# Early, parked products for two z2 tiles, with their weights loaded first: one core, attention plus gMLP

## The chip, the cores and the metric

The kernel runs on one core of one Trainium2 chip. Times are device microseconds of that core; one profiled execution's *span* is about 1.7 us shorter than its time. Engines: PE (TensorE matmul), PEld (weight load, overlapped with PE), DVE (VectorE), ACT (ScalarE), POOL (GpSimd), SP (the queue that issues most DMA). A ratio below is the mean time of one kernel's fast runs over the mean time of the fast runs of the kernel before in the same rounds, so it is not quite the ratio of the medians quoted. A run is called slow when it is over 1.5% above the fastest of its kernel.

## The reference, cut to what matters

```python
xn = layernorm(x)                          # x: 2048 x 512, 16 token tiles of 128
qkv = xn @ wqkv                            # windowed attention: 8 slots, dilation 2
z = gelu(xn @ w_in)                        # w_in: 512 x 1376
z1, z2 = z[..., :688], layernorm(z[..., 688:])
g = w_sp @ z2 + b_sp                       # w_sp: 2048 x 2048
out = x + attention(q, k, v) @ wo + (z1 * g) @ w_out
```

Every token tile is normalised, transposed to `xnT`, and multiplied by the q/k, v, z1 and z2 weights. A z2 tile goes from PSUM through gelu on ACT, with its sum, then a square with its sum, and is normalised later.

## The kernel before

The schedule is manual: each engine runs its instructions in program order. Token tile `4*tb + j` is tile `(j, tb)`; block `j` is the four tiles with that `j`. Only block 0's first two tiles go through first, since their x comes first. The parts that matter:

```python
# DMA issue order on SP (first x tiles ahead of this)
load_wqk(SP, 0)                     # half of the q/k weights, 512 KB
SP.dma_start(xall[:, 1], xblk[1])   # x block 1, 512 KB
load_wqk(SP, 1)                     # second half, 512 KB
for j in range(2, 4):
    SP.dma_start(xall[:, j], xblk[j])
SP.dma_start(w_z2[:], ...)          # 688 KB, last

def zmm(i, wz):                     # L207: 8 matmuls of 344 columns into one "mm" buffer
    pz = ps_mm.tile([P, 2, TBS], F32, name="pz", tag="mm")     # ps_mm has 3 buffers
    ...
def z2_gelu(i, pz):                 # L213, ACT, frees the PSUM buffer
def z2_sq(i):                       # L219, ACT
def z2s(j, tb):
    i = blk(j)[tb]
    z2_gelu(i, zmm(i, w_z2)); z2_sq(i)
def qk_mm(j, c):                    # L264 matmuls into an "mm" buffer, L269 copy on ACT
    pq = qk_tile(); qk_part(pq, j, c, 0, TB); qk_copy(pq, j, c)

warm_up(9)                          # matmuls on a constant tile
... # layernorm of tile (0,0)
tr_copy(t0[0], tr(t0[0])); warm_up(2)
tr_copy(t0[1], tr(t0[1]))
... # q/k products of blocks 0 and 1, layernorm of blocks 1 to 3 on DVE
z2s(0, 0)
z2s(0, 1)
for c in range(C):                  # four q/k products of block 2
    qk_mm(2, c)
... # logits, products on DVE (prod_c L287, prod_w L297), v, z1, then the g stage
```

## Time and profile before

Before the prediction: 210.8 us, median of 3 runs (210.47 to 211.88).

| what | value | from |
|---|---|---|
| PE busy | 202.7 us, 97% of the span | page, busy times |
| the chain before 11.34 us | DMA of the second q/k half, 6.68 us | chain of waits |
| the chain after it | PE, without a hole of note | chain of waits |
| two z2 tiles on PE | 2.41 us | chain of waits |
| gelu and square of one z2 tile on ACT | 1.63 us | ACT timeline |

Three lines of the page of the kernel before; the last gives the busy tenths of PE in 40 equal slices.

```profile
span 209.3 us, 4186 instructions
...
PE 202.7 (97%) x1727; PEld 121.3 (58%) x1731; DVE 176.9 (85%) x267; ACT 92.9 (44%) x148; POOL 5.7 (3%) x21
...
PE   7799999999999999999999999999999999999993
```

The chain of waits of the kernel before, in its first 40 us: start, duration, what, and the number of instructions merged.

```profile
4.61 6.68 DMA r_w<-in_A_wqkv_dram
11.29 0.05 issue
11.34 2.36 PE pq L264 x20
13.69 0.45 PE pt L193 x8
14.14 9.57 PE pq L264 x72
23.71 2.41 PE pz L207 x16
26.12 1.73 PE pq L264 x8
27.84 0.01 issue
27.85 5.34 PE pq L264 x24
```

From 11.34 us each PE piece begins where the last ended. The hole to fill lies before.

The ACT timeline of the kernel before (start, duration, instruction).

```profile
25.67 1.28 ACT L213 ACT_TABLE_LOAD   x1
26.96 0.74 ACT L213 ACTIVATE z<-pz 128x688 bf16<-128x688 f32 x1
...
28.61 0.72 ACT L213 ACTIVATE z<-pz 128x688 bf16<-128x688 f32 x1
...
30.23 0.99 ACT L269 CAST r_qk<-pq 128x1024 bf16<-128x1024 f32 x1
```

The first gelu ends, with its 0.19 us accumulator read from 27.60, at 27.79 us. PE's second q/k product of block 2 needs that buffer and starts at 27.85.

### The profile page before, as it was taken

The numbers are of one execution on the slowest core, as the hardware profiler recorded it, in microseconds if no ns is written. First come the engines' busy times: TensorE is split into PE (matmuls) and PEld (weight loads), VectorE is DVE, ScalarE is ACT, GpSimd is POOL, SyncE is SP. The second block draws the span as 40 slices with busy tenths as digits, with TensorE's granted clock in tenths as the row PEclk, the third lists the DMA queues.
The fourth block names the chain that finished last, engine by engine and source line by source line (L and its number), as shares of the span: only waits on it lengthen the run. The fifth ranks groups of instructions, "written<-read, shape, count | busy, mean of one in ns | idle before, by whom it ended". The sixth has DMA issues, their size and how long they took to land.

```text
span 209.3 us, 4186 instructions
## 1 busy us (share of the span) xinstructions
PE 202.7 (97%) x1727; PEld 121.3 (58%) x1731; DVE 176.9 (85%) x267; ACT 92.9 (44%) x148; POOL 5.7 (3%) x21
## 2 busy tenths in 40 slices
PE   7799999999999999999999999999999999999993
PEld 2578644545566566666666666456666446664441
DVE  3888997969999987999999999859999979991404
ACT  3475797788997897941431223102123102231000
POOL 7000001100000000000000000000000000000000
PEclk9999999999999999999999999999999999999999
DMA  4984556000000499799999776994833234424153
GB/s 132 326 281 66 101 94 232 0 0 3 0 3 0 103 179 210 146 280 216 177 191 218 129 161 145 147 194 150 126 76 89 47 94 150 47 45 89 51 152 100
DMA packets 66914, 25.91 MB, mean 124 GB/s; under 512 B 56080, under 2 KB 66768, under 8 KB 66768
## 3 DMA queue, kind: packets, MB, share of 16 engines
q1 hardware_dynamic: 66304, 25.20, 56.1%
q10 hardware_dynamic: 592, 0.46, 0.7%
q8 instruction: 13, 0.21, 0.4%
q14 instruction: 5, 0.04, 0.1%
HBM read 10.13 MB, written 2.10 MB: 58 GB/s over the span
## 4 chain that ended last, share of the span: by engine, by line
PE 93%; DMA 3%; SPq 2%; issue 1%; DVE 0%; DVEq 0%
PE pg L377 36%; PE pz L207 18%; PE pq L264 12%; PE po L430 7%; PE po L411 7%; PE pv L342 7%; PE pl L304 4%; DMA r_w<-in_A_wqkv_dram 3%; PE pa L430 1%; PE po L417 1%; SPq L138 1%; SPq L131 1%; SPq L147 0%; PE pt L193 0%; DVE r_qk L422 0%
## 5 line engine op out<-in xcount | busy, mean ns | idle before, releaser
L377 PE MATMUL pg<-z,r_qk 128*128 128x344 bf16 x512 | 76.8, 309 | 0.0
L377 PEld LDWEIGHTS <-r_qk 128*128 128x128 bf16 x512 | 50.0, 98 | 24.9 <-issue 0.4
L207 PE MATMUL pz<-w_z,xnT 128*128 128x344 bf16 x256 | 40.9, 309 | 0.0
L380 ACT ACTIVATE gs<-pg,b_col 128x688 bf16<-128x688 f32 x16 | 13.3, 832 | 57.0 <-PE pg L377 50.1
L353 DVE TENSOR_TENSOR r_pr<-r_x,r_w 128x2048 bf16<-128x2048 bf16 x32 | 38.1, 1221 | 0.3
L357 DVE TENSOR_TENSOR r_pr<-r_pr 128x2048 bf16<-128x2048 bf16 x28 | 33.8, 1219 | 0.1
L207 PEld LDWEIGHTS <-xnT 128*128 128x128 bf16 x256 | 24.6, 98 | 14.7 <-issue 2.0
L264 PE MATMUL pq<-xnT,r_w 128*128 128x256 bf16 (+1 forms) x176 | 29.4, 321 | 0.8 <-ACT xnT L197 0.7
L297 DVE TENSOR_TENSOR r_pr<-r_qk 128x2048 bf16<-128x2048 bf16 x24 | 27.5, 1218 | 2.8 <-ACT r_qk L269 2.8
L264 PEld LDWEIGHTS <-r_w 128*128 128x128 bf16 x176 | 16.8, 98 | 11.5 <-issue 1.8
L422 DVE TENSOR_TENSOR r_qk<-po,r_qk 128x512 bf16<-128x512 f32 x14 | 9.0, 686 | 15.6 <-PE po L430 15.6
L256 ACT ACTIVATE z1u<-pz 128x688 bf16<-128x688 f32 x16 | 11.9, 742 | 20.8 <-PE pz L207 20.7
L269 ACT CAST r_qk<-pq 128x1024 bf16<-128x1024 f32 x16 | 15.8, 1012 | 5.8 <-PE pq L264 4.3
L430 PE MATMUL po<-r_w,uT 128*128 128x512 bf16 x66 | 14.9, 379 | 0.6 <-issue 0.6
L342 PE MATMUL pv<-xnT,r_w 128*32 128x512 bf16 x256 | 14.7, 380 | 0.0
L411 PE MATMUL po<-r_lg,r_pr 32*128 32x512 bf16 x224 | 14.5, 375 | 0.0
L430 PEld LDWEIGHTS <-uT 128*128 128x128 bf16 x80 | 7.5, 98 | 10.2 <-issue 1.7
L175 DVE BATCH_NORM_STATS2 stats<-r_x 128x6 f32<-128x512 bf16 x16 | 10.8, 672 | 2.3 <-DMA r_x<-in_A_x_dram 2.1
L219 ACT ACTIVATE junk<-z 128x688 bf16<-128x688 bf16 x16 | 12.4, 778 | 0.5
L213 ACT ACTIVATE z<-pz 128x688 bf16<-128x688 f32 x16 | 11.8, 736 | 1.9 <-PE pz L207 1.9
L342 PEld LDWEIGHTS <-r_w 128*32 128x32 bf16 x256 | 9.5, 139 | 4.5 <-issue 0.3
L411 PEld LDWEIGHTS <-r_pr 32*128 32x128 bf16 x256 | 6.2, 93 | 7.7 <-issue 1.3
(67 smaller groups left out, 136.3 us busy)
## 6 DMA issues: line engine op xcount, KB each, us to landing
r_lg<-in_A_wo_dram SPq DMA_DIRECT2D x4, 512.0 KB, 9.0
r_qk<-in_A_x_dram SPq DMA_DIRECT2D x16, 128.0 KB, 2.2
out_dram<-r_qk SPq DMA_DIRECT2D x15, 128.0 KB, 1.7
r_x<-in_A_x_dram SPq DMA_DIRECT2D x3, 512.0 KB, 6.0
w_z<-in_B_w_in_dram SPq DMA_DIRECT2D x2, 688.0 KB, 5.3
r_w<-in_A_wqkv_dram SPq DMA_DIRECT2D x4, 256.0 KB, 6.4
r_w<-in_B_w_out_dram SPq DMA_DIRECT2D x1, 640.0 KB, 5.6
r_w<-in_A_wqkv_dram SPq DMA_DIRECT2D x1, 512.0 KB, 4.0
```

What stands on the lines that cost most here:

```text
L207: PE.matmul(pz[:, hh, 0:FHALF], xnT[:, kc, i * P:(i + 1) * P], wz[:, kc, hh * FHALF:(hh + 1) * FHALF], start=(kc == 0), stop=(kc == C - 1))
L219: A.activation(junk[:], z2[:, i, :], ACT.Square, accum_out=zsq[:, q:q + 1])
L264: PE.matmul(pq[:, s, b0 * P:b1 * P], wqk[:, kc, s * D + c * P:s * D + (c + 1) * P], xv[:, kc, b0:b1, j, :], start=(kc == 0), stop=(kc == C ...
L269: A.copy(dst[:, :, :, j, :], pq[:].rearrange("p s (b t) -> p s b t", b=TB))
L297: V.tensor_tensor(pr[g % 2][:, :, ww], q4, k4, ALU.mult)
L342: PE.matmul(pv[32 * tb:32 * tb + 32, dd, :], wv[:, kc, 2 * d2 + dd, :], xnT[:, kc, tb * TBS:(tb + 1) * TBS], start=(kc == 0), stop=(kc == ...
L353: V.tensor_tensor(pw_t[n], vp[:, :, off:off + P], a_sb[:, slot_w(w), ts].unsqueeze(1).broadcast_to([P, DH, P]), ALU.mult)
L357: V.tensor_tensor(pw_t[n] if dst is None else dst, pw_t[n], pw_t[m], ALU.add)
L377: PE.matmul(pg[:, hh, 0:FHALF], wsp[n % NWSP][:, k, :], z2[:, k, hh * FHALF:(hh + 1) * FHALF], start=(q == 0), stop=(q == NT - 1))
L380: A.activation(gs[:], pg[:, :, 0:FHALF], ACT.Identity, bias=b_col[:, i:i + 1])
L411: PE.matmul(pos[tb], op[32 * tb:32 * tb + 32, d, o * P:(o + 1) * P], wo_r[32 * tb:32 * tb + 32, d, :], start=(d == 0), stop=False, tile_po ...
L430: PE.matmul(pos[tb], uT[:, o % 2, m, tb * P:(tb + 1) * P], wout[:, m, :], start=False, stop=(m == MCH - 3))
```

## The change

The intent: PE has a hole while it waits for q/k weights. Load the z2 weights first, multiply the first two token tiles by them in that hole, copy the products to SBUF in fp32 (the gelu table is not loaded yet, square root's is), and put them through gelu at the old place. The parking space is part of the logits tile, which is not in use yet. Later z2 tiles move up by two places. The diff, with cuts:

```diff
     load_x0(A, 3)
+    SP.dma_start(w_z2[:], B_w_in[:, FH:F]...)
     load_wqk(SP, 0)
     SP.dma_start(xall[:, 1], xblk[1])
     load_wqk(SP, 1)
     for j in range(2, 4):
         SP.dma_start(xall[:, j], xblk[j])
-    SP.dma_start(w_z2[:], B_w_in[:, FH:F]...)
...
+    z2raw = r_lg[:, 0:2 * FH].rearrange("p (n a b) -> p n a b", n=2, a=2)
+    def z2_park(n, i):
+        pz = zmm(i, w_z2)
+        A.copy(z2raw[:, n], pz[:, :, 0:FHALF])
+    def z2_parked(n, i):
+        A.activation(z2[:, i, :]..., z2raw[:, n], ACT.Gelu_apprx_tanh, accum_out=zsum[:, q:q + 1])
+        z2_sq(i)
...
         tr_copy(t0[n], tr(t0[n]))
-        if n == 0:
-            warm_up(2)
...
+    z2_park(0, t0[0])
+    z2_park(1, t0[1])
+    tr_copy(t0[2], tr(t0[2]))
+    tr_copy(t0[3], tr(t0[3]))
     pqs = [qk_tile() for _ in range(3)]
-    qk_part(pqs[0], 0, 0, 0, 2)
-    tr_copy(t0[2], tr(t0[2]))
-    qk_part(pqs[1], 0, 1, 0, 2)
-    tr_copy(t0[3], tr(t0[3]))
-    qk_part(pqs[2], 0, 2, 0, 2)
+    for c in range(3):
+        qk_part(pqs[c], 0, c, 0, 2)
...
-    z2s(0, 0)
-    z2s(0, 1)
+    z2_parked(0, t0[0])
+    z2_parked(1, t0[1])
+    z2s(0, 2)
+    z2s(0, 3)
     for c in range(C):
         qk_mm(2, c)
... (the later z2s calls each move up by two)
```

More of the change, by code (lines that the diff above doesn't have):

```diff
@@ L145 @@
     load_x0(A, 3)
+    SP.dma_start(w_z2[:], B_w_in[:, FH:F].rearrange("(k p) f -> p k f", p=P))
     load_wqk(SP, 0)
@@ L150 @@
         SP.dma_start(xall[:, j], xblk[j])
-    SP.dma_start(w_z2[:], B_w_in[:, FH:F].rearrange("(k p) f -> p k f", p=P))
     V.memset(warm[:], 0.0)
@@ L439, in out_mm @@
                     store(tb, SP, slice(0, D))
+    z2raw = r_lg[:, 0:2 * FH].rearrange("p (n a b) -> p n a b", n=2, a=2)
[3 more added lines that the diff above has]
+    def z2_parked(n, i):
+        q = 4 * (i % 4) + i // 4
+        A.activation(z2[:, i, :].rearrange("p (a b) -> p a b", a=2), z2raw[:, n],
+                     ACT.Gelu_apprx_tanh, accum_out=zsum[:, q:q + 1])
+        z2_sq(i)
     pwm = ps_aux.tile([P, TBS], F32, name="pwm", tag="aux")
@@ L551 @@
     prods(3)
-    qk_mm(3, 0)
-    z2s(0, 2)
-    qk_mm(3, 1)
-    qk_mm(3, 2)
-    z2s(0, 3)
+    for c in range(3):
+        qk_mm(3, c)
+    z2s(1, 0)
     logits(2)
     qk_mm(3, 3)
-    z2s(1, 0)
+    z2s(1, 1)
     prods(4)
@@ L565 @@
     v_mm(0)
-    z2s(1, 1)
     z2s(1, 2)
+    z2s(1, 3)
     logits(4)
@@ L571 @@
     v_mm(1)
-    z2s(1, 3)
     z2s(2, 0)
+    z2s(2, 1)
     logits(5)
@@ L576 @@
     v_mm(2)
-    z2s(2, 1)
     for n in range(4):
```

## The prediction

> **What bounds the kernel now.** The page's busy table gives PE 97% of a 209.3 us span, and the chain of waits is PE without a gap from 11.34 us to the end (0.5% issue). Before 11.34 us the chain is DMA: the second half of the q/k weights, issued at 4.06 us, lands at 11.29 us (one SP queue, packets nearly in order). So only two things count: when the dense PE run starts, and whether the run stays dense.
>
> **What the change moves.**
> 1. Two z2 tiles of eight-matmul pairs (chain of waits: 16 matmuls, 2.41 us) leave the dense run and go into the hole before it: gain 2.4 us. So do two warm-up matmuls.
> 2. The 688 KB of w_z2 go ahead of both q/k halves and of x block 1. DMA packets then moved about 290 to 340 KB per us, so these land some 2.1 us later: the second half near 13.4 us. The parked products need w_z2 (about 7.6 us) and take until about 10; two transposes and two q/k partials follow and still fit before 13.4. So the dense run starts about 2.1 us later. Loss 2.1 us: the front is nearly a wash. x block 1 also lands later, so VectorE's layernorm chain slips 1.3 to 2 us, no more than PE.
> 3. ScalarE gets two PSUM copies (about 0.75 us each), where it has room.
> 4. ScalarE's gelu and square of the parked tiles stay where they were, right after the table load (25.67 us before), but PE now goes on with tiles (0,2) and (0,3), whose gelus queue behind them. The timeline shows 1.63 us of ScalarE per tile there (gelu starts at 26.96, 28.61, next copy 30.23): 3.3 us more ahead of the first PSUM release. The Trainium skill ("TensorE: Matmul & The Clock Gate", table at the top) calls ScalarE's queue strict FIFO; this trace shows its instructions in program order. PE has three such PSUM buffers: two z2 tiles and one q/k product fill them. Before, gelu of (0,0) freed its buffer at 27.79 us and PE took it at 27.85: no slack at all. So I expect a PE stall of about 2.9 us (2.2 to 3.3) before the second q/k product of block 2.
>
> **Sum on the critical path.** -2.4 + 2.1 + 2.9 = +2.6 us. Later nothing gives it back: PE was dense there. The VectorE products slip by about 3.5 us and logits(4) to (7) had 0.6 to 2.4 us of slack, but PE slips too, so further stalls are tenths at most.
>
> **Clock.** The same page, Part 1, says the clock opens after a busy window of about 3.4 us. Here it opened at about 7.5 us (matmuls of 512 columns took about 0.43 us before). Without the two warm-ups it may open one window later; the parked products would then take up to 4.6 us, costing about 0.5 us more.
>
> **Prediction.** 213.3 us, range 211.2 to 215.3. Faster by over 2%: 0.01; within 2%: 0.86; slower by over 2%: 0.13.
>
> **What would show it.** Right: the q/k weight DMA still heads the chain; one PE idle of 2 to 3 us on a q/k product released by ScalarE's gelu from PSUM, near 30 us; VectorE idle near 37 us growing from 1.1 to over 2 us; PE as dense as before after 40 us. Wrong: no such PE idle, or weights landing by 12 us.
>
> **What would make it wrong.** Weights that land hardly later (then about 211.5); a cold clock for longer; VectorE falling so far behind that logits wait (then 215 and above).

## The result, and the profile after

The changed kernel took 216.81 us, median of 4 runs (215.04 to 217.49), against 210.93 us; the ratio of fast runs is 1.0262 (95% interval 1.0212 to 1.0312). It is slower by 2.6%, where 1.2% was expected, and lies above the stated range. The profile is of the fastest of the four runs, so it shows the loss at its smallest.

The same lines of the page, after, with the granted PE clock (in tenths) added.

```profile
span 213.3 us, 4188 instructions
...
PE 204.1 (96%) x1729; PEld 121.2 (57%) x1729; DVE 176.9 (83%) x267; ACT 94.4 (44%) x150; POOL 4.9 (2%) x21
...
PE   7799959999999999999999999999999999999993
...
PEclk9999996999999999999999999999999999999999
```

One slice of PE is down to 5, and the slice after it has a clock of 0.6. PE's busy time has grown by 1.4 us, though it does two warm-up matmuls less.

The PE timeline after; the bracket gives the idle time before a group and what ended it.

```profile
7.68 2.49 PE L207 MATMUL pz<-w_z,xnT 128*128 128x344 bf16 x16 [0.85 <-DMA w_z<-in_B_w_in_dram]
...
24.97 2.50 PE L207 MATMUL pz<-w_z,xnT 128*128 128x344 bf16 x16
27.50 1.89 PE L264 MATMUL pq<-xnT,r_w 128*128 128x512 bf16 x8
32.51 7.03 PE L264 MATMUL pq<-xnT,r_w 128*128 128x512 bf16 x24 [3.12 <-ACT z L213]
```

The parked products run at 7.68 us. Block 0's other z2 tiles begin at 24.97, where the chain before had this step at 23.71 (23.54 in its timeline). Then PE waits 3.12 us for a gelu to free a PSUM buffer, and the 24 matmuls that took 5.34 us before now take 7.03.

The ACT timeline after.

```profile
27.00 1.28 ACT L450 ACT_TABLE_LOAD   x1
28.30 0.78 ACT L450 ACTIVATE z<-r_lg 128x688 bf16<-128x688 f32 x1
...
29.98 0.76 ACT L450 ACTIVATE z<-r_lg 128x688 bf16<-128x688 f32 x1
...
31.64 0.72 ACT L213 ACTIVATE z<-pz 128x688 bf16<-128x688 f32 x1
```

The two parked tiles hold ACT from 28.30 to 31.64 us, 3.34 us, ahead of the first gelu that frees a buffer.

Stretches of time of the two kernels (PE, PEld, DVE, ACT, POOL busy, then the granted clock), before first.

```profile
29.00:33.00 4.00, 4.00 (x20) 1.69 (x18) 4.00 (x4) 3.73 (x7) 0.00 (x0) 1.00 0.60 154
33.00:38.00 5.00, 5.00 (x50) 2.54 (x50) 3.87 (x5) 3.40 (x5) 1.29 (x2) 1.00 0.44 157
```

```profile
29.00:33.00 4.00, 0.88 (x5) 0.35 (x4) 4.00 (x5) 3.91 (x11) 0.00 (x0) 1.00 0.51 96
33.00:38.00 5.00, 5.00 (x17) 1.94 (x16) 2.89 (x3) 3.92 (x9) 0.42 (x2) 0.66 0.69 240
```

Between 33 and 38 us PE is fully busy in both, but after the change it gets through 17 matmuls instead of 50 (some are of other kinds, so this is only an impression) at a clock of 0.66.

The sum for this trace: +1.43 us (z2 tiles of block 0 start at 24.97 instead of 23.54), +3.12 (idle), +1.69 (7.03 for 5.34), -2.41 (two tiles moved out of the dense run) = +3.83. The spans differ by 4.0. The first, second and fourth terms had been foreseen, the third not.

### The profile page after: what moved, and what is told of

It is laid out like the page before. It is cut to its first block, busy times and chain, and to the rows that moved or that the text cites. A ratio compares the mean times of both kernels' runs of the same rounds, so it can differ in the third digit from the quotient of the medians.

```text
span 213.3 us, 4188 instructions
## 1 busy us (share of the span) xinstructions
PE 204.1 (96%) x1729; PEld 121.2 (57%) x1729; DVE 176.9 (83%) x267; ACT 94.4 (44%) x150; POOL 4.9 (2%) x21
## 4 chain that ended last, share of the span: by engine, by line
PE 86%; DVE 4%; ACT 4%; DMA 2%; SPq 1%; issue 0%; DVEq 0%
PE pg L377 35%; PE pz L207 17%; PE pq L264 8%; PE po L430 7%; PE po L411 7%; PE pv L342 7%; PE pl L304 4%; DMA w_z<-in_B_w_in_dram 2%; DVE stats L175 2%; ACT r_qk L269 1%; PE pa L430 1%; DVE r_x L186 1%; ACT junk L219 1%; PE po L417 1%; ACT z L450 1%; DVE mv L176 1%
## 5 line engine op out<-in xcount | busy, mean ns | idle before, releaser
L264 PE MATMUL pq<-xnT,r_w 128*128 128x256 bf16 (+1 forms) x176 | 30.6, 333 | 3.2 <-ACT z L213 3.1
L430 PE MATMUL po<-r_w,uT 128*128 128x512 bf16 x70 | 15.8, 380 | 0.0
L213 ACT ACTIVATE z<-pz 128x688 bf16<-128x688 f32 x14 | 10.3, 734 | 1.5 <-PE pz L207 1.5
```

The lines of the kernel that those rows point to most:

```text
L264: PE.matmul(pq[:, s, b0 * P:b1 * P], wqk[:, kc, s * D + c * P:s * D + (c + 1) * P], xv[:, kc, b0:b1, j, :], start=(kc == 0), stop=(kc == C ...
L430: PE.matmul(pos[tb], uT[:, o % 2, m, tb * P:(tb + 1) * P], wout[:, m, :], start=False, stop=(m == MCH - 3))
```

## The experiments

The theory (called A): the static sum of the forecast is right, and what is missing is the PE clock, which the changed kernel loses at up to two places, after the stall near 30 us and at the front, differently from run to run. Rivals: the load order is the main cause; the clock is a bystander and DMA timing varies; VectorE's delay makes PE wait later. All outputs are right. Kernels of one batch share a chip and the runs of the kernel before. The three batches had before at 210.71, 210.65 and 210.80 us.

### a0: the changed kernel again

No edit.

> The changed kernel unedited, to see its spread. Theory A (a PE stall of 3.1 us closes the clock, and how long it stays closed differs from run to run): times from about 215 to 217.5 us, and runs with a lower mean granted clock (0.984) are about 1.7 us longer than runs at 0.992. Theory B (the clock is a bystander and the kernel simply varies with DMA timing): time and mean granted clock unrelated.

Measured: 215.91 us (213.51 to 218.19), ratio of fast runs 1.0178. Its runs, with the mean granted clock that goes with each:

| time, us | clock | state |
|---|---|---|
| 213.51 | 1.000 | fast |
| 214.82, 215.03 | 0.992 | fast |
| 216.79, 216.93, 218.19 | 0.984 | slow |

The ratio leaves the three slow runs out, so it understates this kernel. Even among the fast runs, one closed window more (a fall of 0.008 in the mean is 3.4 us at half clock in 213 us) goes with 1.3 to 1.5 us. The run without such a loss stands at +2.8 us over before, close to the forecast's +2.6. As theory A has it, time and clock go together. The trace of this label (a slow run) has the clock open at 4.51 us, closed from 7.93 to 11.34 us, while the parked products take 4.14 us instead of 2.49, and closed again from 35.23 to 38.65 us.

Across all the runs the pairing is looser than in this table. Four runs are slow for their mean clock: 216.51 us at 1.000 among the four runs of the result, 216.29 at 1.000 in e1, 213.53 at 0.999 in e3 and 212.89 at 1.000 in f4. A clock that first opens late does not show in this mean (see e1), which may be behind the first three; no trace of any of the four was kept, so their cause stays open.

### e1: keep PE busy in the stall

```diff
-    for c in range(C):
+    qk_mm(2, 0)
+    pkw = ps_aux.tile([P, TBS], F32, name="pkw", tag="aux")
+    for _ in range(13):
+        PE.matmul(pkw[:], warm[:, 0:P], warm[:], start=True, stop=True)
+    for c in range(1, C):
         qk_mm(2, c)
```

> Changed kernel plus 13 idle-time matmuls of 512 columns on a constant tile between the first and second q/k product of block 2, some 2.8 us of PE work inside the 3.1 us stall; nothing else moves. Theory A (half of the loss beyond the forecast is the clock that the stall closes): granted clock stays 1.0 from the front on, the 24 matmuls after the stall take about 5.2 to 5.3 us instead of 7.0, and the time falls to about 213 us (1.7 us or more below the changed kernel, ratio to before about 1.010 to 1.013) with less spread. Theory B: no gain, or a loss, about 215 to 217 us.

Measured: 215.31 us (214.71 to 216.29), ratio 1.0221. The clock after the stall did what was expected; the time did not fall to 213. PE timeline of e1:

```profile
7.78 3.90 PE L207 MATMUL pz<-w_z,xnT 128*128 128x344 bf16 x16 [0.80 <-DMA w_z<-in_B_w_in_dram]
...
26.34 2.50 PE L207 MATMUL pz<-w_z,xnT 128*128 128x344 bf16 x16
28.69 1.89 PE L264 MATMUL pq<-xnT,r_w 128*128 128x512 bf16 x8
30.63 2.75 PE L562 MATMUL pkw<-warm 128*128 128x512 bf16 x12
33.88 5.34 PE L264 MATMUL pq<-xnT,r_w 128*128 128x512 bf16 x24 [0.49 <-ACT z L213]
```

(The trace holds records of 12 of the 13 filler matmuls.) The 24 matmuls are back at 5.34 us. But in this run the clock first opened at 10.68 us, so the parked products took 3.90 us and the z2 tiles of block 0 started at 26.34 us, 1.37 later than in the changed kernel's first profile. That is the second place: the front. Three of the five runs have a mean clock of 0.991, so they lost a window after the first opening although the stall was filled; a0's trace shows such a loss at the front (7.93 to 11.34 us), but no trace of these three was kept.

### e2: only the load order

```diff
 (kernel before)
+    SP.dma_start(w_z2[:], ...)
     load_wqk(SP, 0)
     ...
-    SP.dma_start(w_z2[:], ...)
```

> The kernel before with only the z2 weights moved ahead of the q/k weights; no parking. My front theory: the second q/k half lands about 1.5 to 2 us later, nothing fills the hole, and the whole chain moves with it: about 212.5 us (1.4 to 2 us slower, ratio 1.007 to 1.010). Rival (the load order is the main cause of the slowdown): 214 us or more, ratio 1.015 or above. If the longer hole keeps the clock closed for another 3.4 us window, up to 1.7 us on top, and the trace will show it.

Measured: 213.96 us (212.63 to 214.86), ratio 1.0154. By its ratio this meets the rival's line (1.015 or above), by its median it stays just short of it (214). The chain of its profiled run (212.76 us, clock open from 7.27 us):

```profile
6.00 7.14 DMA r_w<-in_A_wqkv_dram
13.14 0.05 issue
13.19 2.36 PE pq L264 x20
```

With an open clock the dense run begins at 13.19 instead of 11.34, +1.85 us, and the two fastest runs (212.63 and 212.76, clock 0.999 and 1.000) are 1.9 to 2.1 us slower than before: the front theory's size. The other four, at mean clocks of 0.984 to 0.991, take 213.62 to 214.86. So the longer hole seems to cost clock as well; only the mean clocks say so, as no trace of these four was kept. The load order alone thus costs much of the changed kernel's loss; there the parked work pays part of it back.

### e3: the parked gelus later

The parking space moves to columns of the logits tile that are written later, so that the gelus can wait:

```diff
-    z2_parked(0, t0[0])
-    z2_parked(1, t0[1])
     z2s(0, 2); z2s(0, 3)
 ...
     qk_mm(3, 0)
+    z2_parked(0, t0[0])
     qk_mm(3, 1)
     qk_mm(3, 2)
+    z2_parked(1, t0[1])
     z2s(1, 0)
```

> Changed kernel with the two parked gelus and squares moved on ScalarE to after the q/k copies of block 2 (behind the first and third q/k copies of block 3), parked in columns of the logits tile that are written later still. Theory A (the whole loss beyond the front is ScalarE's 3.3 us of parked work ahead of the first PSUM release): no PE stall near 30 us, clock 1.0 throughout, time about 209.5 to 210.5 us, ratio 0.993 to 0.999, so slightly faster than before: 2.4 us moved out against 1.4 us of later start. Rival (the delay is from the later weights or VectorE): still 213 us or more.

Measured: fast runs from 211.76 to 213.53 us (212.41 is the median of all six), ratio 1.0079. That is well below the changed kernel's 215.91, but short of the expected win, with mean clocks between 0.989 and 0.999 where 1.0 was expected. (Its slowest fast run, 213.53 us, has the highest mean clock of the five fast runs.) One of the six runs, the profiled one, took 1204.97 us. In its trace the nine warm-up matmuls took 11.86 us instead of 4.02, and PE's matmuls kept to a slow pace to the end (the group of 512 g matmuls averaged 1273 ns against 309). It is a slow run whose cause stays open; no run of the same schedule with a warmer front (f3, twice) repeated it, and nothing here rests on it.

### f0 and f1: the front kept busy, without and with the filler in the stall

The front filler, the same in f0, f1, f3, f4 and f5:

```diff
-    warm_up(9)
+    warm_up(10)
 ...
         tr_copy(t0[n], tr(t0[n]))
+        if n == 0:
+            warm_up(3)
```

f0 is the changed kernel with it, f1 is e1 with it.

> Changed kernel with the front kept busy: one more warm-up matmul before the first transposes and three (the kernel before had two) between the transposes of the first and second tile; everything else as changed. Theory A2 (the changed kernel is hit by the clock twice: at the front, where taking out the two warm-ups and waiting for the z2 weights often leaves the clock closed for one more 3.4 us window, and after the stall): the parked products always run at 2.5 us, the stall still closes the clock for 3.4 us; about 214.5 to 215.2 us, with the spread of the plain changed kernel (213.5 to 218.2) gone to under 1 us above the low end. Rival (only the stall matters): unchanged median near 216.

> Both fillers: the front kept busy and the 13 idle-time matmuls in the stall. Theory A2: clock open from about 7 us to the end, what remains is the static sum, about 1.4 later start + 3.1 stall - 2.4 moved out, so 212.7 to 213.3 us, ratio 1.009 to 1.013, small spread. If something else than the clock makes the difference between the forecast 213.3 and the measured 216: still 214.5 or more.

Medians of the four kernels (the upper row ran on one chip, the lower on another, with medians of before of 210.71 and 210.65 us):

| | stall left idle | stall filled |
|---|---|---|
| front as changed | 215.91 (213.51 to 218.19) | 215.31 (214.71 to 216.29) |
| front filled | 215.52 (213.62 to 217.86) | 213.30 (213.10 to 213.90) |

f1's ratio is 1.0131. With both fillers the kernel takes the forecast 213.3 us, and the spread is 0.8 us instead of 4.7. The fillers do no useful work, so what they bring back was lost to the clock. Either alone brings little in the median; with five or six runs a kernel I can't say how the two losses combine. PE timeline of f1 (its profiled run took 213.68 us):

```profile
25.28 2.50 PE L207 MATMUL pz<-w_z,xnT 128*128 128x344 bf16 x16
...
29.56 2.75 PE L564 MATMUL pkw<-warm 128*128 128x512 bf16 x12
32.82 5.34 PE L264 MATMUL pq<-xnT,r_w 128*128 128x512 bf16 x24 [0.51 <-ACT z L213]
```

f0 misses its own expectation: 215.52 us and a spread of 4.2 us are nearer to the rival's "unchanged median near 216" than to a spread of under 1 us.

f0's fast runs again: 213.62 and 213.82 at clocks of 0.999 and 1.000, 215.30, 215.74 and 215.93 at 0.992. The sixth, a slow one, took 217.86 at 0.984; its trace was not kept. In f1, with the stall filled, no run is below 0.997, nor is any of f3, f3_again, f4 and f5 with the same front filler (29 runs in all). So the front loses no window there after the first opening, and it is the stall that takes the clock in f0. The same stall sometimes closes it and sometimes doesn't, which my expectation ("still closes the clock") had wrong. The profiled run of f0 (213.82) is one where it did not. The waits of its PE between 20 and 45 us, and the group that follows the stall:

```profile
PE pq L264 <- ACT z L213: 3.3, 1, 3.3
```

```profile
33.00 5.34 PE L264 MATMUL pq<-xnT,r_w 128*128 128x512 bf16 x24 [3.29 <-ACT z L213]
```

The idle is 3.3 us, a little more than in the changed kernel's first profile, yet the clock stayed open and the 24 matmuls took 5.34 us. The clock's steps in each trace lie on a grid of 3.413 us; for each trace I took the grid from the clock's first step and worked out the share of each window in which a matmul of PE was running:

```
trace   window ends at   PE busy share   the clock then
after   33.51 us         0.29            closes
a0       7.93            0.36            closes
a0      35.23            0.28            closes
f0      31.38 and 34.79  0.51 and 0.52   stays open
e2      10.69            0.51            stays open
f4      31.50            0.60            stays open
before   7.26            0.82            opens
after    6.21            0.81            opens
e1       7.27            0.74            stays closed until 10.68 (0.85)
```

An idle that falls mostly in one window closes the clock, and the same idle divided between two windows does not. Where the grid lies differs from run to run, and so does the time. This is read from a handful of windows: between 0.36 and 0.51 nothing was seen. At the front, the kernel before opened the clock at 7.26 us (the forecast said about 7.5) with 0.82, and e1, which like the changed kernel lacks the two warm-ups, missed at the same instant with 0.74. (Transposes are counted as busy here. Without them the windows that opened in before and after stand at 0.70 and 0.73, below the 0.76 of warm-up matmuls alone in the window of before that ends at 3.85 us and did not open; so if one share decides, transposes count.)

### f3: front filled and gelus late

e3 with the front filler.

> Front kept busy and the parked gelus and squares late (no stall). Theory A2: no PE idle of over 0.5 us after the start of the dense run, clock open throughout, the gain of 2.4 us against about 1.4 us of later start: 209.4 to 210.3 us, ratio 0.994 to 0.998, a small win over the kernel before. Rival (the load order costs as much as the parking saves): 210.7 us or above.

Measured: 210.57 us (210.06 to 211.31), ratio 0.9995; repeated in the last batch as f3_again:

> The same kernel as f3, on the same chip as f5, for a fair comparison: 210.2 to 210.8 us, within 0.3% of the kernel before.

Measured: 210.84 us, ratio 0.9998. There is no stall in its trace, and its clock stays open. The PE waits of f3 from 8.6 us to 205 us, all of them, show it; the first is the wait before the parked products, which begin at 8.55 us:

```profile
PE pz L207 <- DMA w_z<-in_B_w_in_dram: 1.3, 1, 1.3
PE po L430 <- issue: 0.6, 4, 0.2
PE pl L304 <- DVE r_pr L297: 0.2, 1, 0.2
```

So with both mistakes mended, the idea itself gains nothing that these runs can show: f3 lies between the win that I expected (up to 210.3 us) and the rival's line (210.7), f3_again beyond that line and 0.04 us above its own range. The z2 tiles of block 0 begin at 25.83 us in f3 and 25.53 in f3_again, 2.3 and 2.0 us later than before, against the 2.41 us moved out.

### f4: front filled, only the squares late

```diff
 (z2_parked without its z2_sq)
-    z2s(0, 2); z2s(0, 3)
+    for tb in range(2, 4):
+        i = blk(0)[tb]; z2_gelu(i, zmm(i, w_z2))
     for c in range(C):
         qk_mm(2, c)
+    for tb in range(4):
+        z2_sq(blk(0)[tb])
```

> Front kept busy; of the parked work only the two gelus stay ahead of the first PSUM release, all four squares of block 0 go behind the q/k copies of block 2. Theory A2: the PE stall shrinks from 3.1 us to about 1.4 us, which is too short to close the clock (a window is 3.4 us), so the cost falls by both the 1.7 us and the re-throttle's 1.7: about 211 to 212 us. Rival (the clock closes at any stall there): the gain is 1.7 us only, 213 us or more, and the trace shows a closed clock after 33 us.

Measured: 211.88 us (211.77 to 212.89), ratio 1.0065. The PE waits of f4 between 20 and 45 us:

```profile
PE pq L264 <- ACT z L213: 1.4, 1, 1.4
```

The stall follows ACT's work ahead of the first release. No run of f4 has a mean clock below 0.997: 1.4 us of idle closed the clock in none of the six, 3.1 to 3.3 us often did. Against f0 the median falls by 3.6 us for 1.9 us less idle.

### f5: the z2 weights in two halves

f3, with the z2 weights loaded as two halves of 344 columns, and both parked tiles multiplied by the first half while the second is on its way:

```diff
+    for hh in range(2):
+        SP.dma_start(w_z2h[:, hh], B_w_in[:, FH + hh * FHALF:FH + (hh + 1) * FHALF]...)
 ...
+        for hh in range(2):
+            for pz, i in zip(pzs, tiles):
+                ... PE.matmul(pz[:, hh, 0:FHALF], ..., w_z2[:, kc, hh, :], ...)
```

> The best kernel so far (front kept busy, parked gelus late), with the z2 weights loaded as two halves of 344 columns, and both tiles multiplied by the first half while the second is on its way. In all five traces of parking kernels with an open front clock the z2 matmuls of block 0 begin 17.3 us after the first parked matmul (7.68 and 24.97, 8.18 and 25.46, 8.01 and 25.28, 8.55 and 25.83, 7.93 and 25.21). If the landing of the z2 weights is what sets that, an earlier first half moves all by up to about 1 us: 209.6 to 210.2 us, a small win. If the later q/k weights or VectorE's layernorm chain stand right behind it, the gain is 0.3 us at most: 210.2 us or more, the same as before.

Measured: 210.64 us (210.28 to 210.93), ratio 0.9986 (0.9965 to 1.0007), the same as before. PE timeline of f5:

```profile
7.20 2.76 PE L452 MATMUL pz<-w_z,xnT 128*128 128x344 bf16 x16
...
13.19 2.36 PE L267 MATMUL pq<-xnT,r_w 128*128 128x256 bf16 x20 [0.24 <-DMA r_w<-in_A_wqkv_dram]
```

The parked work starts earlier, at 7.20 us, and PE then waits for the second q/k half, at 13.19 us as in e2. The front is set by how soon the bytes come: 688 KB moved ahead cost about what they let PE do. No version clearly beat the kernel before.

## Why the prediction was wrong

- **The mechanism near 30 us was right.** A stall of about 2.9 us (2.2 to 3.3) was forecast; it measured 3.12 in the first profile, and e3 and f3, which take ACT's parked work away from there, have none.
- **The front was right in kind.** A shift of +2.1 us was forecast; +1.4 to +2.3 was measured where the clock was open (24.97 to 25.83 against 23.54). In detail it was wrong: the chain's head is the z2 weights' DMA until 7.68 us, then PE and VectorE's layernorm chain, not the q/k weights. Only f5, where the parked work starts earlier, has the q/k weights at its head again.
- **The static sum was right.** f1 has the same data flow and stall, with the clock kept open, and takes 213.30 us against the forecast 213.3. That it agrees to the tenth is luck: in f1's trace the front costs 1.74 us (25.28 against 23.54) where 2.1 was forecast, and the wait with its filler lasts 3.3 us (29.50 to 32.82) where 2.9 was, so two errors of 0.4 us cancel.
- **The step that failed is "Clock".** The forecast looked at the clock only at the front, and priced one window at "about 0.5 us more". It gives no reason; as I read it, the second q/k half, due near 13.4 us, was to hide the rest. But PE hardly awaited that half (0.2 us, by its weight load, in the first profile), and e1's late opening moved everything by 1.37 us. And it forecast an idle of 2.9 us in a warm PE without asking what that does to the clock, though the page it cited warns of it. The stall let the clock close for 3.4 us, which made 5.34 us of matmuls into 7.03, +1.7. The mis-sized term is thus the clock's: 0.5 us as forecast, 2.6 us as measured between the medians of a0 and f1 (215.91 and 213.30, on two chips whose before medians differ by 0.06). On one chip, from f0 to f1, the stall's part alone is 2.2 us.
- **VectorE did not cause it.** Its idle before the block 2 products grew from 1.1 to 4.75 us, more than forecast, but PE had no further stall: its list of waits from 38 to 205 us is empty in the changed kernel's first profile. The chain back from the end of the stall does run through VectorE's layernorms (15.73 to 24.85 us), but what follows them on ACT starts 1.33 us later than before (24.87 against 23.54), no more than PE's own 1.43. Whether a faster VectorE would have shortened the stall was not tested.
- **The probabilities followed the same error.** 0.13 for slower by over 2% left out that a stall near the length of a clock window makes the outcome depend on the run.

The Trainium skill ("TensorE: Matmul & The Clock Gate", section "Why this matters for your kernels") warns against PE idle gaps of over about 3 us between bursts. The first profile agrees with it: 3.12 us idle, then 3.4 us at half clock. The same page (Part 1) gives the window as 3413 ns and free-running; the traces show steps on a grid of 3.413 us at a phase that differs per run. The strict order of ScalarE's queue, which the forecast took from the table at the top of that page, is what every ACT timeline here shows. The forecast used that page for the start of the kernel alone.

## What to carry to other kernels

When a change adds a PE wait to a dense run, price the wait and then ask about the clock: here 3.1 us of idle cost 4.8 us in the first profile (3.12 + 1.69), while 1.4 us of idle left the clock open. Before moving work into a hole, see that its later half (here the gelu on ACT, in program order) does not land ahead of something PE waits for, and that the bytes moved ahead for it don't cost what the hole gives. Where times spread, set each run's time beside its mean clock, and look in a trace for when the clock first opened.

## What the Trainium skill lacked or had wrong

- "TensorE: Matmul & The Clock Gate", Part 1, says the clock closes after an idle window of about 3.4 us. Here windows that were not idle closed it: PE was busy in 0.28, 0.29 and 0.36 of the three windows that ended in a closing, while 0.51, 0.52 and 0.60 kept it open. The page has no such share.
- The same page says the clock opens after a busy window. Here shares of 0.81 and 0.82 opened it and 0.74 and 0.76 did not (transposes counted as busy). The page gives no share.
- Neither that page nor another that I read says that an idle of fixed length closes the clock or not by how it falls on the window grid: idles of 3.1 and 3.3 us, closed in the first profile of the changed kernel and open in that of f0; 4 of f0's 6 runs have a mean clock of 0.992 or less, while f1, with the stall filled, has none below 0.997.
- No page that I read warns that a mean granted clock counts only from the first recorded step: e1's profiled run shows 0.998, though its clock first opened at 10.68 us and its parked products took 3.90 us instead of 2.49.
- The page on TensorE, Part 1, has seen the clock stuck at a quarter for over 50 us. e3's run of 1204.97 us may be such a case, but far longer: its g matmuls averaged 1273 ns against 309 in a span of 1203 us, with no clock step in its records.
